# First key products kept plain, weight bits on ScalarE, values double-buffered: one edit of a fused attention and MoE kernel

## The chip, the cores and the metric

One core of a Trainium2 chip runs the whole program. The metric is device microseconds from launch to end; lower is better. TensorE (PE) multiplies matrices, VectorE (DVE), ScalarE (ACT) and GpSimd (POOL) work element by element, and SyncE (SP) only issues DMA transfers here. Each engine executes its own instructions in the order in which the program was written, so a waiting instruction holds up everything behind it on that engine.

## What is computed

Three layers in a row, all in float32:

```python
# 1. delta-rule attention, 4 batches x 8 heads, 768 tokens, head size 48
k_n = k / (norm(k) + 1e-06)
for t in range(768):
    y[t]  = q[t] @ state
    v_old = state.T @ k_n[t]
    state = state + beta[t] * outer(k_n[t], v[t] - v_old)
# 2. gated MLP: x is (3072, 384), d_ff 2048
h = x @ w_in;  x = (h * sigmoid(1.702 * h)) @ w_out
# 3. four dense experts of width 1024, mixed by normalised domain_probs
out += p[:, e:e+1] * (relu(x @ w1[e]) @ w2[e])
```

## The kernel before, in words

**Attention.** The 768 tokens are cut into 12 chunks of 64 (`u`, 0 to 11), and two chunks form a batch `w` (0, 2, 4, ...). For each chunk TensorE forms the products of keys with keys (`queue_g`, L523) in two halves of eight head groups, and VectorE keeps the 32x32 diagonal blocks of them (`keep_d`, L558) in a scratch buffer `GG`, while the off-diagonal blocks are copied out to `G` (`keep_x`). The blocks are turned so that each of the 128 partitions holds one 32x32 triangle, the triangle is inverted row by row, and it is turned back (`to_rows`, L639). For the later batches this inversion runs on GpSimd (`queue_inverse`, L597: 30 steps of two operations, L619 and L621). For batch 0 it runs on VectorE (`queue_first_inverse`, L644): two 16x16 triangles side by side in 14 steps (L674, L676), which are then merged by two rounds of small matmuls (`first` L718, `out1`, `second` L727, `out2` L732). A chunk then solves for its update, reads its output `y` and updates the state (`queue_chain`, L754).

The key norms come from `queue_keys` (L365): a square on ScalarE (L393), a sum (L396) and a chain of about 14 small VectorE operations (L408 to L433) that ends in `rates`. For batch 0 the diagonal blocks are multiplied by a constant mask `cmask` on their way out of PSUM (chunk 0: L564, each half in four pieces of 32 partitions; chunk 1: L571, each half in one piece). For later batches `premask` (L511) builds mask times weight beforehand and `keep_d` multiplies by that.

**Scratch.** Four buffers `scr` (L323) are handed out by `claim`. The squares, `GG`, the turned triangle `X` (kept until both chunks of the batch have solved), the turned copy `d` of the first inverse, and a part of `y` on its way out (`YS`) all live there.

**Weights of the MLP.** The 16 weight tiles arrive as 64-bit numbers, 128x1536 words each. `queue_w1` (L251) turns each into a float32 pair: `small` (L286, ScalarE) and `low` (L289, VectorE, a shift right by 29) work on the two words, `shift` (L293, VectorE) joins them, `hi` (L298, ScalarE) rounds and `lo` (L301, VectorE) keeps the remainder.

**MLP and experts.** The token tiles `t` have 512 columns. For tile 0 and tile 1 the first layer starts on half tiles (256 columns) as soon as one chunk's `y` is there (`HALVED`, `items` L1133, `split_stage` L1142). Each of the 16 (MLP) or 8 (expert) steps `f` is nine matmuls into `ph` (L1013), a gate on ScalarE and VectorE (L1123, L1125, L1126) and nine matmuls into `px` (L1108). The experts (L1279 on) follow when attention is over.

**What sets the order.** The order of the program is not written out by hand. A planner (`Order` and `Task`, L28 to L147) keeps a clock for each engine, a cost, a priority `prio` (lower goes first) and dependencies for each task, and writes a task's instructions at the moment when its clocks say that the task could start. Tasks that name two engines go to the one that would end first, with a bonus for the first named. `can` says when a scratch buffer or PSUM bank is free. MLP matmuls drive the clock (`tick`, L68), attention tasks are slipped in between, and `until` (L76) lets attention run freely while the MLP has to wait. SP's DMA queue is one of the engines ("HW"). What the chip then does differs from the planner's clocks, but the order on each engine stays as written.

Of the kernel before, what the change touches and what calls it, by code (L numbers as in the profile page):

```python
# [9 lines left out]
I32 = mybir.dt.int32  # L10
AF = mybir.ActivationFunctionType
# [5 lines left out]
C = 64  # L17
SB = 32
# [6 lines left out]
GW = 1  # L25
# [62 lines left out]
class Task:  # L88
    def __init__(self, order, fn, eng, cost, deps, lat, prio, slack, can, extra):
        self.o, self.fn, self.lat, self.prio, self.slack, self.can = order, fn, lat, prio, slack, can  # L90
        self.engs = dict(zip(eng, cost)) if isinstance(eng, tuple) else {eng: cost}
        self.pe = eng == "PE"
        self.extra = extra
# [36 lines left out]
    def issue(self):  # L130
# [13 lines left out]
        if len(self.engs) > 1:  # L144
            self.fn(e)
        else:
            self.fn()  # L147
# [3 lines left out]
def delta_attention_moe_moe_kernel(  # L151
# [55 lines left out]
    cmask = ap_.tile([128, SB], F32, name="cmask")  # L207
# [43 lines left out]
    def queue_w1(f, after):  # L251
# [111 lines left out]
    NR = {}  # L363
# [88 lines left out]
    def queue_q(u):  # L452
# [8 lines left out]
        lq = task(load, "HW", 1.32, (edone.get(u - 2), normed[u] if u > 1 else None), lat=4.8, prio=p if u < 4 else p - 30, slack=5)  # L461
        ends, visits, masks = [], [], []
        whole = 1 if u < 2 else 2
        for o in range(2):
# [18 lines left out]
            if len(visits) == whole:  # L483
                t = task(lambda fs=tuple(visits): weave(fs), "PE", 1.0 if whole == 1 else 1.3,
                         (*placed[u], lq, begun[0], *(ends[-1:] if u > 1 else ())), prio=p + 1,
                         can=lambda: None if u > 1 and not od.moe else some_free(banks(), whole))
                for c, f in masks:
                    c.setdefault("end", []).append(task(f, "DVE", 0.6, (t,), prio=p + 1))
                    ends.append(c["end"][-1])
# [16 lines left out]
    def queue_premask(us):  # L506
# [11 lines left out]
        premasked[w] = task(premask, ("POOL", "DVE"), (1.2 * len(us), 0.6 * len(us)), (normed[w],), prio=p,  # L518
# [4 lines left out]
    def queue_g(u):  # L523
# [6 lines left out]
        whole = 1 if u < 4 else 2  # L530
        for o in range(2):
# [3 lines left out]
            def gram(o=o, cell=cell, flip=flip):  # L535
# [4 lines left out]
                for i in range(8):  # L540
                    g = 2 * i + o
                    if u < GW:
                        for x in range(2):
                            d, r = DR[x], TR[x]
                            mm(ps[r:r + C, i, :], lhsT=kr[d:d + D, g, :], rhs=kr[d:d + D, g, :], start=True, stop=True)
                            yield
                        continue
# [10 lines left out]
            def keep_d(x, o=o, cell=cell, flip=flip):  # L558
                if w not in GG:
                    GG[w] = scr[claim(SCR, gheld[w]["end"])][:, 0:2 * NP * SB].rearrange("p (g i) -> p g i", i=SB)  # L560
                a = rows(o)[0]
                if u < GW:
                    for r in range(0, 128, SB):
# [814 lines left out]
```

## Time and profile before

| | |
|---|---|
| median of 3 runs | 1409.41 us (1405.75 to 1409.59) |
| the profiled execution, its own time | 1406.45 us |
| its span, first to last instruction | 1404.7 us |
| PE busy | 1354.4 us (96%) |
| VectorE, ScalarE, GpSimd busy | 617.5, 421.2, 202.5 us |
| TensorE clock granted, mean | 0.991 |

The rows below come from one profiled execution. Times are microseconds from the start of the span. "L564" is line 564 of the kernel; "out<-in" names the tiles. In a timeline, the first number is the start, the second the time from the first to the end of the last of the merged instructions, and a bracket gives idle time of that engine just before and what ended it. A busy share says how full an engine is in a stretch and not whether it sets the end.

### The profile page before, as it was taken

How to read it: one execution, taken by the hardware profiler on the slowest of the kernel's cores; microseconds unless marked ns; L12 is line 12 of the kernel's file. 1: busy time of each engine (PE TensorE's matmuls, PEld its weight loads, DVE VectorE, ACT ScalarE, POOL GpSimd, SP SyncE). 2: the span in 40 equal slices, each digit the busy share in tenths (PEclk: the TensorE clock that was granted, in tenths of full speed). 3: DMA queues.
4: the chain of work that ended last, by engine and by line, in shares of the span. 5: the costliest groups of instructions: out<-in, count | busy, mean ns of one | idle time of the engine just before them, and what ended most of it. 6: DMA issues, size and time to landing. Idle time of an engine off the chain costs nothing.

```text
span 1404.7 us, 29499 instructions
## 1 busy us (share of the span) xinstructions
PE 1354.4 (96%) x13072; PEld 1144.5 (81%) x13072; DVE 617.5 (44%) x1035; ACT 421.2 (30%) x797; POOL 202.5 (14%) x355
## 2 busy tenths in 40 slices
PE   5699999998999999999999999999999999999998
PEld 4588789986878788878888888888888888888888
DVE  7879466474363423323333224443233433233343
ACT  2564344352342434422222112222122222111111
POOL 3057543603507200000000000000000000000000
PEclk9999989999999999999999999999999999999999
DMA  8550131222020103201100001010001000011111
GB/s 222 171 173 17 28 96 40 61 62 61 12 61 7 39 5 134 68 0 29 33 30 30 8 1 30 31 38 31 1 19 30 31 31 8 0 30 31 31 30 46
DMA packets 53696, 63.39 MB, mean 45 GB/s; under 512 B 37120, under 2 KB 38592, under 8 KB 53568
## 3 DMA queue, kind: packets, MB, share of 16 engines
q1 hardware_dynamic: 53568, 61.50, 15.4%
q8 instruction: 102, 1.67, 0.5%
q14 instruction: 26, 0.21, 0.1%
HBM read 52.58 MB, written 7.91 MB: 43 GB/s over the span
## 4 chain that ended last, share of the span: by engine, by line
PE 92%; DVE 4%; issue 2%; DMA 1%; ACT 1%; SPq 0%; DVEq 0%; ACTq 0%
PE ph L1013 42%; PE po L1235 23%; PE px L1108 14%; PE po L1265 5%; PE y L849 2%; PE ch L820 1%; PE gp L550 1%; PE ch L806 1%; PE ch L872 1%; PE ch L835 1%; PE gp L473 1%; DMA rw<-in_w_dram 1%; DMA k<-in_k_dram 0%; ACT su L183 0%; DMA kt<-in_kt_dram 0%
## 5 line engine op out<-in xcount | busy, mean ns | idle before, releaser
L1013 PE MATMUL ph<-xs,w 128*128 128x512 f32 (+1 forms) x2808 | 657.5, 377 | 3.6 <-ACT xs L183 2.0
L1013 PEld LDWEIGHTS ph<-xs,w 128*128 128x128 f32 x2808 | 504.1, 190 | 96.7 <-ACT xs L183 2.1
L1296 DVE SCALAR_TENSOR_TENSOR hh<-ph,hh 128x512 fp32r<-128x512 f32 x192 | 132.5, 690 | 503.4 <-ACT hh L1295 503.4
L1235 PE MATMUL po<-hh,w 128*128 128x512 f32 x1440 | 352.4, 389 | 0.0
L1235 PEld LDWEIGHTS po<-hh,w 128*128 128x128 f32 x1440 | 270.4, 188 | 56.0
L1295 ACT ACTIVATE hh<-ph 128x512 fp32r<-128x512 f32 x192 | 114.9, 598 | 616.6 <-PE ph L1013 616.6
L1108 PE MATMUL px<-gh,w 128*128 128x512 f32 (+1 forms) x1080 | 231.6, 354 | 2.3 <-DVE gh L1126 2.1
L1108 PEld LDWEIGHTS px<-gh,w 128*128 128x128 f32 x1080 | 177.3, 190 | 30.4 <-DVE gh L1126 3.0
L1126 DVE TENSOR_TENSOR gh<-ph,gh 128x512 fp32r<-128x512 f32 (+1 forms) x120 | 69.9, 582 | 149.0 <-ACT gh L1125 147.8
L1123 ACT ACTIVATE ph<-ph 128x512 f32<-128x512 f32 (+1 forms) x120 | 59.6, 497 | 184.9 <-PE ph L1013 179.8
L621 POOL TENSOR_TENSOR scr<-scr,itmp 128x30 f32<-128x30 f32 (+9 forms) x150 | 85.0, 567 | 11.8
L619 POOL TENSOR_TENSOR itmp<-scr 128x30 f32<-128x30 f32 (+9 forms) x150 | 80.4, 536 | 11.1
L1265 PE MATMUL po<-w,hh 128*128 128x384 f32 x384 | 73.9, 342 | 0.0
L1265 PEld LDWEIGHTS po<-w,hh 128*128 128x128 f32 x384 | 69.3, 188 | 2.4
L1125 ACT CAST gh<-ph 128x512 fp32r<-128x512 f32 (+1 forms) x120 | 60.2, 502 | 3.8
L183 ACT COPY su<-ch 64x384 f32<-64x384 f32 (+2 forms) x85 | 38.1, 458 | 49.9 <-PE ch L820 48.5
L1095 DVE TENSOR_TENSOR xs<-x,xs 128x512 fp32r<-128x512 f32 x72 | 45.3, 684 | 0.0
L1094 ACT CAST xs<-x 128x512 fp32r<-128x512 f32 x72 | 39.7, 619 | 0.0
L813 DVE TENSOR_TENSOR v<-v,ch 128x384 f32<-128x384 f32 (+1 forms) x56 | 30.1, 551 | 17.5 <-PE ch L835 5.1
L478 DVE TENSOR_TENSOR pq<-gp,pmask 64x512 f32<-64x512 f32 x48 | 33.1, 689 | 5.9 <-PE gp L473 5.1
L243 DVE TENSOR_TENSOR w<-raw,w 128x768 fp32r<-128x768 f32 x32 | 30.7, 958 | 10.3 <-ACT w L242 9.5
L768 POOL TENSOR_TENSOR v<-v,nr 128x768 f32<-128x768 f32 x9 | 13.3, 1479 | 127.2 <-DMA v<-in_v_dram 119.1
(118 smaller groups left out, 765.8 us busy)
## 6 DMA issues: line engine op xcount, KB each, us to landing
raw<-in_we_dram SPq DMA_DIRECT2D x32, 384.0 KB, 3.0
rw<-in_w_dram SPq DMA_DIRECT2D x14, 768.0 KB, 5.7
raw<-prd SPq DMA_DIRECT2D x20, 256.0 KB, 3.2
kt<-in_kt_dram SPq DMA_DIRECT2D x24, 192.0 KB, 5.1
k<-in_k_dram SPq DMA_DIRECT2D x12, 384.0 KB, 6.1
pq<-in_q_dram SPq DMA_DIRECT2D x24, 192.0 KB, 4.2
v<-in_v_dram SPq DMA_DIRECT2D x12, 384.0 KB, 3.1
out_dram<-oacc SPq DMA_DIRECT2D x80, 48.0 KB, 1.7
```

The costliest lines, as they stand in the source:

```text
L619: E.tensor_tensor(out=tv, in0=x[:, j:j + 1, j + 1:].broadcast_to([128, m, r]), in1=x[:, 0:m, j:j + 1].broadcast_to([128, m, r]), op=ALU.mult)
L621: E.tensor_tensor(out=x[:, 0:m, j + 1:], in0=x[:, 0:m, j + 1:], in1=tv, op=ALU.add)
L1013: mm(ps, lhsT=w[:, a, kk * 128:(kk + 1) * 128], rhs=xs[kk][:, b, cs], start=kk == 0 and i == 0, stop=kk == KD - 1 and i == 2)
L1095: nc.vector.tensor_tensor(out=s[:, 1, :], in0=src, in1=s[:, 0, :].bitcast(F32), op=ALU.subtract)
L1108: mm(px[d][:, cs], lhsT=w[:, a, 384 + d * 128:384 + (d + 1) * 128], rhs=gh[:, b, 0:cs.stop - cs.start], start=f == 0 and i == 0 and cs.sta ...
L1123: a = task(lambda: nc.scalar.activation(out=ph, in_=ph, func=AF.Gelu_apprx_sigmoid), "ACT", 0.05 + 0.43 * c, (pe,), **kw)
L1125: a = task(lambda: nc.scalar.copy(out=hi, in_=ph), "ACT", 0.05 + 0.43 * c, (a,), **kw)
L1126: a = task(lambda: nc.vector.tensor_tensor(out=lo, in0=ph, in1=hi.bitcast(F32), op=ALU.subtract), "DVE", 0.07 + 0.53 * c, (a,), **kw)
L1235: mm(po[kk], lhsT=w[:, a, 384 + kk * 128:384 + (kk + 1) * 128], rhs=hh[:, c, :], start=f == 0 and i == 0, stop=f == F2 - 1 and i == 2)
L1265: mm(ps, lhsT=hh[:, a, b * 128:(b + 1) * 128], rhs=w[:, c, 384:768].rearrange("p (k a i) -> p a k i", a=4, k=KD), start=f == 0 and i == 0, ...
L1295: nc.scalar.activation(out=hh[:, 0, :], in_=ph, func=AF.Relu)
L1296: nc.vector.scalar_tensor_tensor(out=hh[:, 1, :], in0=ph, scalar=0.0, in1=hh[:, 0, :].bitcast(F32), op0=ALU.max, op1=ALU.subtract)
```

## The change

- **First keys.** For chunks 0 and 1 the key products are formed as for later chunks (both halves woven, on all four quadrants), and the diagonal blocks are copied out of PSUM unmasked, by ScalarE or VectorE (`keep_raw`). Mask and weight come together in a tile `m`, made by GpSimd or VectorE (`weigh`) once the norms are there, and are multiplied in after the turn (`clear`, which also clears one more corner).
- **Constants.** The masks and zeroed tiles are made by eight GpSimd tasks of the planner, in the order j, q0, pm, h, su, st, q1, g. `cmask` is gone. What uses one of them names it as a dependency. The helpers' home is a tile `spare` in a weight slot.
- **Low bits.** `low` moves from VectorE (shift right) to ScalarE (scale by 2^-29, rounded down).
- **Values.** `v` has two buffers, so chunk u's load follows the solve of chunk u-2. From chunk 2 on VectorE alone scales `v`; for chunks 0 and 1 GpSimd or VectorE.
- **Scratch.** Three buffers instead of four.
- **Planner's figures.** Several costs, among them the GpSimd inverse (factor 1.5 to 1.2 for batch 2, 1.0 to 0.95 for later ones).

```diff
         def low():
-            nc.vector.tensor_scalar(out=cell["lo"], in0=cell["lo"], scalar1=29, scalar2=None,
-                                    op0=ALU.logical_shift_right)
+            nc.scalar.activation(out=cell["lo"].bitcast(U32), in_=cell["lo"].bitcast(U32), func=AF.Copy, scale=2.0 ** -29 * (1 - 2.0 ** -16),
+                                 bias=7.5 * 2.0 ** -16 - 0.5)
...
-            b = task(low, "DVE", 0.6, (dep, begun[0]), **kw)
+            b = task(low, "ACT", 0.9, (dep, begun[0]), **kw)
...
-    scr = [ap_.tile([128, NP * C], F32, name=f"scr{i}") for i in range(4)]
+    scr = [ap_.tile([128, NP * C], F32, name=f"scr{i}") for i in range(3)]
...
-    SCR = (0, 1, 2, 3)
+    SCR = (0, 1, 2)
...
-        lq = task(load, "HW", 1.32, (edone.get(u - 2), normed[u] if u > 1 else None), lat=4.8, prio=p if u < 4 else p - 30, slack=5)
+        lq = task(load, "HW", 1.32, (edone.get(u - 2), normed[u] if u > 1 else zeros[f"q{u}"]), lat=4.8, prio=p if u < 4 else p - 30, slack=5)
...
-        whole = 1 if u < 4 else 2
+        whole = 1 if u in (2, 3) else 2
...
+            def keep_raw(e, x, o=o, cell=cell, flip=flip):
                 if w not in GG:
                     GG[w] = scr[claim(SCR, gheld[w]["end"])][:, 0:2 * NP * SB].rearrange("p (g i) -> p g i", i=SB)
                 a = rows(o)[0]
-                if u < GW:
-                    for r in range(0, 128, SB):
-                        V.tensor_tensor(out=GG[w][r:r + SB, o:NP:2, :] if not u else GG[w][r:r + SB, NP + o:2 * NP:2, :], in0=cell["ps"][r:r + SB, :, r % C:r % C + SB],
-                                        in1=cmask[r:r + SB].unsqueeze(1).broadcast_to([SB, 8, SB]), op=ALU.mult)
-                    return
                 r, n = (0, 128) if x is None else (TR[x], C)
                 s = 0 if x is None else half(x, flip)
...
+                copy(e, GG[w][r:r + n, c * NP + o:(c + 1) * NP:2, :], cell["ps"][s:s + n, :, a:a + SB])
...
-            last = task(lambda j=j: step(j), "POOL", (0.52 + 0.0037 * m) * (1.5 if w == 2 else 1.0), (last,), prio=p)
+            last = task(lambda j=j: step(j), "POOL", (0.52 + 0.0037 * m) * (1.2 if w == 2 else 0.95), (last,), prio=p)
...
+        def weigh(e):
+            bt = BT[w].rearrange("p (h i) -> p h i", h=2)
+            cell["m"] = spare[:, H * H:3 * H * H].rearrange("p (h a b) -> p h a b", h=2, a=H)
+            for h in range(2):
+                (V if e == "DVE" else nc.gpsimd).tensor_tensor(
+                    out=cell["m"][:, h], in0=jmask, in1=bt[:, h].unsqueeze(1).broadcast_to([128, H, H]), op=ALU.mult)
+
         def clear():
 
             x = cell["x"]
-            bt = BT[w].rearrange("p (h i) -> p h i", h=2)
-            V.tensor_tensor(out=x, in0=x, in1=bt.unsqueeze(2).broadcast_to([128, 2, H, H]), op=ALU.mult)
+            V.tensor_tensor(out=x, in0=x, in1=cell["m"], op=ALU.mult)
             V.memset(X[w][:, H:, 0:H], 0.0)
+            V.memset(X[w][:, 0:H, H:], 0.0)
             V.memset(X[w].rearrange("p i j -> p (i j)")[:, 0:SB * SB:SB + 1], 1.0)
...
         begun[w] = task(begin, "DVE", 2.0, ds, prio=p, can=lambda: any_free(SCR))
-        last = task(clear, "DVE", 1.1, (begun[w],), prio=p)
+        last = task(weigh, ("POOL", "DVE"), (1.2, 0.9), (normed[w], zeros["j"]), prio=0)
+        last = task(clear, "DVE", 1.4, (begun[w], last), prio=p)
...
-        before = [solved2[u - 1, hu] for hu in range(2) if (u - 1, hu) in solved2]
+        before = [solved2[u - 2, hu] for hu in range(2) if (u - 2, hu) in solved2]
...
-            V2[u] = ap_.tile([128, NP, D], F32, name="v2", tag="v2")
+            V2[u] = ap_.tile([128, NP, D], F32, name="v2", tag="v2", bufs=2)
...
-        lv = task(scale_v, ("POOL", "DVE"), (1.9, 0.97), (lv, normed[u]), prio=p + 1)
+        lv = task(scale_v, ("DVE",) if u > 1 else ("POOL", "DVE"), (0.97,) if u > 1 else (1.5, 0.97), (lv, normed[u]), prio=p + 1)
...
+        for n, fn, cost in (("j", set_j, 0.5), ("q0", lambda: E_.memset(PQ[0], 0.0), 1.85), ("pm", set_p, 1.95),
+                            ("h", set_h, 0.9), ("su", lambda: E_.memset(SU, 0.0), 1.4),
+                            ("st", lambda: E_.memset(stage, 0.0), 1.4), ("q1", lambda: E_.memset(PQ[1], 0.0), 1.85),
+                            ("g", set_g, 1.1)):
+            zeros[n] = task(fn, "POOL", cost, (), prio=2)
+        od.clk["POOL"] = 0.8
```

## Rows read from the trace of the kernel before

**Rows 1.** Busy time by stretch: length, PE, PEld, DVE, ACT, POOL, PEclk, DMA share, GB/s.
```profile
0.00:33.07 33.07, 16.00 (x320) 14.55 (x320) 24.12 (x67) 8.69 (x15) 12.68 (x36) 1.00 0.86 227
33.07:66.39 33.32, 19.41 (x865) 17.53 (x865) 27.70 (x56) 17.92 (x36) 2.69 (x1) 1.00 0.51 166
66.39:100.00 33.61, 32.97 (x764) 29.84 (x766) 24.94 (x44) 26.03 (x54) 13.76 (x23) 0.95 0.59 183
100.00:126.00 26.00, 23.44 (x323) 22.30 (x318) 25.53 (x38) 11.66 (x25) 24.04 (x26) 0.93 0.22 48
...
168.00:189.00 21.00, 16.73 (x423) 13.69 (x419) 9.13 (x16) 8.04 (x18) 18.43 (x32) 0.76 0.31 84
...
335.00:600.00 265.00, 264.87 (x2978) 214.56 (x2977) 108.70 (x180) 99.72 (x181) 70.00 (x127) 1.00 0.14 43
```

**Rows 2.** Timeline of VectorE, 11 to 31 us.
```profile
11.03 1.61 DVE L408 TENSOR_SCALAR scr<-scr 128x32 int32<-128x32 int32 x1
...
16.15 1.68 DVE L564 TENSOR_TENSOR scr<-gp,cmask 32x256 f32<-32x256 f32 x4
17.86 0.42 DVE L571 TENSOR_TENSOR scr<-gp,cmask 128x256 f32<-128x256 f32 x1
...
20.29 1.15 DVE L666 TENSOR_TENSOR scr<-scr,bt 128x512 f32<-128x512 f32 x1
...
29.52 0.69 DVE L681 TENSOR_TENSOR scr<-scr,bt 128x512 f32<-128x512 f32 x1
```

**Rows 3.** Timeline: first merge, on TensorE, ScalarE and TensorE again.
```profile
33.22 1.90 PE L718 MATMUL gp<-scr,scr 32*32 32x16 f32 x128 [10.94 <-ACT rw L286]
...
34.91 0.83 ACT L393 ACTIVATE scr<-k 128x768 f32<-128x768 f32 x1
35.77 0.37 ACT L183 COPY scr<-gp 128x256 f32<-128x256 f32 x1
...
39.53 1.57 PE L727 MATMUL gp<-scr,scr 32*32 32x16 f32 x99 [2.73 <-issue]
```

**Rows 4.** Chain and timeline: chunk 2's output lands, tile 1 starts; inverse of batch 2.
```profile
174.27 2.33 DMA stage<-scr
...
180.40 2.07 PE ph L1013 x8
...
132.75 1.92 POOL L625 TENSOR_TENSOR scr<-scr,bt 128x1024 f32<-128x1024 f32 x1
...
149.59 2.23 DVE L642 STREAM_TRANSPOSE scr<-scr 128x1024 f32<-128x1024 f32 x1
```

**Rows 5.** Timeline: GpSimd beside L408, and L408 of the next batch.
```profile
10.80 1.81 POOL L1046 MEMSET pq<- 128x2048 f32 x1
...
54.27 0.18 DVE L408 TENSOR_SCALAR scr<-scr 128x32 int32<-128x32 int32 x1
```

**Rows 6.** Timeline, 60 to 67 us: GpSimd, VectorE, ScalarE.
```profile
60.26 2.69 POOL L514 TENSOR_TENSOR scr<-gmask,bt 128x1024 f32<-128x1024 f32 x1 [39.37 <-DVE bt L432]
61.69 1.68 DVE L289 TENSOR_SCALAR rw<-rw 128x768 int32<-128x768 int32 x1
...
65.14 0.91 ACT L298 CAST w<-rw 128x768 fp32r<-128x768 f32 x1 [3.04 <-DVE rw L293]
66.07 0.60 ACT L183 CAST xs<-y 128x128 fp32r<-128x128 f32 x3
```

**Rows 7.** Groups by line, 66.39 to 126 us: count, busy us, mean ns, idle before.
```profile
L289 DVE TENSOR_SCALAR rw<-rw 128x768 int32<-128x768 int32 x9 | 5.9, 652 | 0.0
...
L286 ACT ACTIVATE rw<-rw 128x768 f32<-128x768 f32 x7 | 6.3, 921 | 0.0
```

**Rows 8.** Timeline and chain: square of chunk 4, turn of batch 2, solve of chunk 1.
```profile
80.65 0.85 ACT L393 ACTIVATE scr<-k 128x768 f32<-128x768 f32 x1
...
82.50 2.04 DVE L610 STREAM_TRANSPOSE scr<-scr 128x1024 f32<-128x1024 f32 x1
...
92.78 0.47 PE ch L820 x32
```

More of the change, by code (lines that the diff above doesn't have):

```diff
@@ L24 @@
 PE_SHARE = 0.8
-GW = 1
 class Order:
@@ L361, in delta_attention_moe_moe_kernel @@
     direct = {}
-    NR = {}
+    NR, zeros = {}, {}
+    spare = wp.tile([128, 1536], F32, name="sp", tag=f"w{RAW - 1}")
+    jmask = spare[:, 0:SB * SB // 4].rearrange("p (a b) -> p a b", a=SB // 2)
     def queue_keys(us):
@@ L558, in keep_d @@
             def keep_d(x, o=o, cell=cell, flip=flip):
+                a = rows(o)[0]
+                r, n = (0, 128) if x is None else (TR[x], C)
+                s = 0 if x is None else half(x, flip)
+                gg = GG[w][r:r + n, c * NP + o:(c + 1) * NP:2, :]
+                V.tensor_tensor(out=gg, in0=cell["ps"][s:s + n, :, a:a + SB], in1=gg, op=ALU.mult)
+            def keep_raw(e, x, o=o, cell=cell, flip=flip):
                 if w not in GG:
@@ L689, in queue_first_inverse @@
                 marks.append(last)
-            last = task(lambda j=j: step(j), "DVE", 0.26 + 0.0042 * j * (H - 1 - j), (last,), prio=p)
+            last = task(lambda j=j: step(j), "DVE", 0.4 + 0.003 * j * (H - 1 - j), (last,), prio=p)
         last = task(end, "DVE", 0.6, (last,), prio=p)
@@ L1039, in delta_attention_moe_moe_kernel @@
-        nc.gpsimd.memset(PQ[0], 0.0)
-        for r in range(0, 128, SB):
-            for o in range(2):
-                nc.gpsimd.affine_select(out=pmask[r:r + SB, o], in_=m2[r:r + SB], pattern=[[1, C]], compare_op=ALU.is_gt,
-                                        fill=0.0, base=-(r % C ^ SB * o), channel_multiplier=-1)
-        nc.gpsimd.memset(SU, 0.0)
-        nc.gpsimd.memset(stage, 0.0)
-        nc.gpsimd.memset(PQ[1], 0.0)
-        od.clk["POOL"] = 9.5
+        H = SB // 2
+        E_ = nc.gpsimd
@@ new lines, in delta_attention_moe_moe_kernel, with set_j, set_g @@
+        ones, minus = spare[:, 1024:1024 + C], spare[:, 1024 + C:1024 + C + SB]
+        def set_j():
+            E_.memset(minus, -1.0)
+            E_.affine_select(out=jmask, in_=minus[:, 0:1].unsqueeze(2).broadcast_to([128, H, H]), pattern=[[-1, H], [1, H]],
+                             compare_op=ALU.is_gt, fill=0.0, base=0, channel_multiplier=0)
+        def set_g():
+            for r in range(0, 128, SB):
+                at = slice(r, r + SB)
+                E_.affine_select(out=gmask[at], in_=minus[at], pattern=[[-1, SB]], compare_op=ALU.is_gt,
+                                 fill=0.0, base=0, channel_multiplier=1)
@@ new lines, in set_h, with set_p @@
+        def set_h():
+            E_.memset(hmask, -1.0)
+            for r in range(0, 128, SB):
+                at = slice(r, r + SB)
+                E_.affine_select(out=hmask[at], in_=hmask[at], pattern=[[0, 1]], compare_op=ALU.is_ge,
+                                 fill=0.0, base=H - 1, channel_multiplier=-1)
+        def set_p():
+            E_.memset(ones, 1.0)
+            for r in range(0, 128, SB):
+                for o in range(2):
+                    E_.affine_select(out=pmask[r:r + SB, o], in_=ones[r:r + SB], pattern=[[1, C]], compare_op=ALU.is_gt,
+                                     fill=0.0, base=-(r % C ^ SB * o), channel_multiplier=-1)
```

46 lines of the change are left out of this document (12 added, 34 removed).

## The prediction

> **What bounds the kernel now.** I read first the table by stretch [rows 1]. From 335 to 600 us TensorE works 264.87 of 265 us at a granted clock of 1.00: it is the bound, and only time in which it stands still or runs slowly can be won. Three places show such time. In the opening (0 to 66.39 us, up to the first MLP matmul) TensorE works 16.00 + 19.41 of 66.39 us, while VectorE works 24.12 + 27.70. From 66.39 to 126 us TensorE idles 0.64 + 2.56 us and the clock averages 0.95 and 0.93; in the second half of that VectorE is busy 25.53 of 26.00 us. From 168 to 189 us TensorE idles 4.27 us at a mean clock of 0.76.
>
> Next I read the timelines, for what holds TensorE in these places. In the opening it is one VectorE chain: L408, the masked copies L564 and L571, the turn, the clear L666, the steps, L681 [rows 2], two more turns, and then the merge matmuls start at 33.22 us [rows 3]. At 168 us it is MLP tile 1, which needs chunk 2's output: its last pieces land at 176.60 us, and the matmuls start at 180.40 [rows 4]. Why so late? GpSimd finished the inverse of batch 2 at 134.67 us (132.75 + 1.92), but VectorE turned it back only at 149.59 [rows 4]. The planner had written the turn that late, since it costs this inverse with a factor of 1.5. Some 15 us lie unused in this chain, and the stop of TensorE hangs on it.
>
> **The change part by part.** 0.3% of the median is 4.2 us, about what a measurement of this kernel can tell from no change.
>
> *First keys.* Between the norms and the turn stand four L564 and one L571, from 16.15 to 18.28 us [rows 2]: 2.1 us leave the chain. In their place come six plain copies, which need only the products and can lie beside the norms. ScalarE is named first for them, and it is busy 8.69 of the first 33.07 us [rows 1]; I cost them at nothing. If that cover fails and three fall to VectorE, they cost 3 x 0.42 = 1.3 us, by L571. Chunk 0 needs twice as many small matmuls as before, on a TensorE that is idle 17 of those 33 us: nothing. The tile `m` is made on GpSimd during the turn: nothing. If it fell to VectorE, its two half-size products would cost about one L681, 0.7 us.
>
> *The clear.* Its product took 1.15 us, while L681 of the same size took 0.69 [rows 2]. With `m` ready I expect 0.69, but one memset is added. Bounds -0.5 and 0, taken -0.2.
>
> *Constants.* L408 took 1.61 us here [rows 2] and 0.18 on the next batch [rows 5]. It ended at 12.64, and the GpSimd memset beside it at 12.61 [rows 5]: it was held by it. In the new order this long memset runs before four short mask pieces, so about one microsecond goes. Bounds -1.43 and 0, taken -1.0. The Trainium skill, "SBUF — State Buffer", section "Who interferes with whom", says that VectorE in a two-port mode and GpSimd hold their shared port as a lock, and that whoever comes second waits out the whole instruction of the other. By that rule L408 would wait for one short piece at most, and the term would be near its bound of -1.43.
>
> *SP's queue.* Loads of q now wait in the planner for their zeroed tile, so the loads behind them (chunk 0's values, the first weights) are issued earlier. Chunk 1's values move ahead of the later weights, which start later by one such load. Nothing, either way: VectorE takes up the first weight only after the inverse.
>
> *Scratch.* With three buffers the square of chunk 2 can't run before the first merge. So it no longer stands in front of the merge's copy, which began at 35.77, behind L393, while its matmuls had ended at 35.12 [rows 3]. A `low` of 0.9 us may stand there instead. Bounds -0.6 and +0.3, taken -0.3. The norms of batch 2 come later by the squares' new place, an estimate of 2 to 3 us (two squares of 0.83 and their sums). L514, which ends that chain, was over at 62.95 [rows 6], and batch 2 is turned at 82.50 [rows 8], with four products in between: covered.
>
> *Low bits.* VectorE loses 16 instructions and ScalarE gains 16. The nearest row for the new price is L286, with the same tile and engine: 0.92 us [rows 7]. One of the old ones sits badly: L289 took 1.68 us beside GpSimd's L514, and ScalarE stood 3.04 us in front of a weight that waited for this, with the conversion of chunk 1's `y` behind it [rows 6]. Bounds -3.0 (all that idle time) and 0; taken halfway, -1.5. From 66.39 to 126 us nine of them, 5.9 us, leave a VectorE that is full in the second half [rows 1, 7]. TensorE can win at most its 3.2 us of idle time and the low clock's share, 0.05 x 33.61 + 0.07 x 26.00 = 3.5 us; I take -2. ScalarE gets nine of 0.92 us. With seven of them (as many as L286 has there) before 100 us it comes to 26.03 + 6.4 = 32.5 of 33.61 us, and the MLP's gates queue behind them: +1. Stretch together -1; bounds -4 and +8.3.
>
> The Trainium skill, "ScalarE: Activation LUTs", section "Rules for kernel authors", speaks against this part: additions and products belong on VectorE, which is the faster per element. The trace agrees on durations, 0.65 against 0.92 us [rows 7]. By that rule the part costs 16 x 0.27 = 4.3 us of engine time, and the sum would be smaller by up to that; by the rows it is paid on the emptier engine.
>
> *Values.* Chunk 1's values are scaled on an idle GpSimd, off the path: nothing. From chunk 2 on, one product of 128x768 per chunk moves to VectorE, which is busy 109 of 265 us there [rows 1]: nothing.
>
> *Planner's figures.* By the formula the 30 steps of this inverse cost 30 x 0.52 + 0.0037 x 4960 = 34 us; a factor of 1.2 instead of 1.5 brings L642 forward by 10.2 us on the planner's clock. From the end of the turn of batch 2 (84.54 [rows 8]) to L642 the chip took 65 us, where the planner counted 51 + 2.4. So it is 12 us on the chip: to about 137 us, just behind GpSimd's end. Then chunk 2's output lands before tile 0 is over, and the stop goes. It is worth 4.27 us of idle time and 0.24 x 21 = 5.0 us of low clock, at most 9.3 us [rows 1]. Attention work that ran inside the stop has still to be done. Taken -7, bounds -9.3 and 0.
>
> *Sum.* Opening -2.1 - 0.2 - 1.0 - 0.3 - 1.5 = -5.1; stretch to 126 us -1; stop -7. Together -13.1 from the profiled execution's 1406.45 us: 1393.4. That execution lies 3.0 us under the median of the three runs, 1409.41; going halfway, I predict **1395 us**.
>
> **The rivals.**
>
> *The stop stays (0.24).* With three buffers the square of chunk 4 (80.65 us) can take the last free one just ahead of the turn of batch 2 (82.50) [rows 8]. The turn then waits for the solve of chunk 1, whose matmuls ended at 93.25: 10.7 us, which eat what the planner's factor gave. For it: the square did come first before. Against it: its priority is the weaker, and ScalarE, which executes it, is fuller now. Then -5.1 - 1 = -6.1 remains, in medians about 1402 us.
>
> *ScalarE becomes the bound (0.10, slower).* It works in order, and each `low` stands in front of gates, state copies and conversions. Its idle time from 66.39 to 100 us was 7.6 us [rows 1], of which my count leaves 1.1; if a late weight or copy uses that up, TensorE waits for every further `low`. With all 16 on the path it is 16 x 0.92 = 14.7 us, and chunk 2 is as late as before, so the stop stays: 1406.45 - 5.1 + 14.7 = 1416, in medians about 1417. The skill's rule for ScalarE leads here.
>
> *The opening isn't VectorE's (0.08).* Between two merge matmuls TensorE stood 2.73 us for nothing that the profile shows [rows 3]. If its instructions come at a pace of their own, an earlier turn only lengthens such stops. With the stop at 168 us left as well, -1 remains: in medians about 1407 us.
>
> **How the numbers follow.** The forecast has 0.58. Low end: the opening with every bound -2.1 - 0.5 - 1.43 - 0.6 - 3.0 = -7.6, the stretch -4, the stop -9.3, from 1406.45: 1385.5, taken 1386. High end: 1408, which takes in the first and the third rival and leaves out ScalarE's 0.10 and a few hundredths around it. Faster than 1405.2 us: the forecast and five sixths of the first rival, 0.78. Within 0.3%: the rest of that and the third, 0.12. Slower than 1413.6 us: 0.10.
>
> **What would show it.** Right, step by step: L408's successor takes well under 1 us; the merge matmuls start by 30 us and the first MLP matmul near 61; batch 2 is turned back within 3 us of GpSimd's last step; TensorE goes from tile 0 into tile 1 without a stop and at a clock of 1.00. Wrong: a turn of batch 2 that starts only after chunk 1's solve; ScalarE over 95% busy for 30 us behind the first MLP matmul, with TensorE waiting for gates; or several microseconds of idle TensorE at the change of tiles.

## The result, and the profile after

| | before | after |
|---|---|---|
| median | 1409.50 us (4 runs, 1405.75 to 1410.40) | 1387.82 us (4 runs, 1387.02 to 1389.33) |
| the profiled execution, its own time | 1406.45 us | 1388.16 us |
| its span | 1404.7 us | 1386.5 us |
| PE busy | 1354.4 us | 1342.3 us |
| TensorE clock granted, mean | 0.991 | 0.998 |

The ratio is 0.9852, with an interval from 0.9833 to 0.9872: faster by 1.5%. Between the two profiled executions the difference is 18.3 us.

To see where the time went, both executions are cut at the same places of the program: the first full run of MLP matmuls, the store of each of the finished MLP tiles 0 to 3 (the moves of `x1d`), and the end. Two of these stretches in the table by stretch of the kernel before, tile 0 and tile 2 (length, PE, PEld, DVE, ACT, POOL busy, clock, DMA share, GB/s):

```profile
67.05:194.57 127.52, 119.44 (x2357) 103.82 (x2358) 89.32 (x149) 63.27 (x134) 80.52 (x126) 0.94 0.26 74
...
292.45:383.98 91.53, 86.69 (x1224) 69.15 (x1222) 44.59 (x79) 32.69 (x64) 33.72 (x63) 0.96 0.18 43
```

The same two of the kernel after:

```profile
64.38:181.00 116.62, 113.54 (x2339) 98.03 (x2343) 83.19 (x141) 63.48 (x133) 76.06 (x124) 0.99 0.32 82
...
274.50:361.74 87.24, 87.16 (x1438) 69.48 (x1437) 50.02 (x86) 33.05 (x65) 30.34 (x55) 1.00 0.20 50
```

| stretch | before | after | difference |
|---|---|---|---|
| opening, to the first full MLP run | 67.05 | 64.38 | -2.67 |
| tile 0 | 127.52 | 116.62 | -10.90 |
| tiles 1 to 3 | 273.21 | 268.30 | -4.91 |
| the rest | 936.92 | 937.20 | +0.28 |

Tile 0 carries most of it: TensorE's idle time there falls from 8.08 to 3.08 us, and the granted clock rises from 0.94 to 0.99, worth about 0.06 x 127.5 - 0.01 x 116.6 = 6.5 us. Within tiles 1 to 3, tile 1 is 4.4 us shorter, tile 2 4.3 us shorter and tile 3 3.8 us longer.

The rows of after that answer to those of before. First, the table by stretch [rows 1]:

```profile
0.00:30.47 30.47, 9.40 (x384) 7.89 (x384) 20.15 (x60) 10.81 (x20) 14.79 (x32) 1.00 1.01 257
30.47:64.40 33.93, 21.87 (x930) 19.50 (x930) 28.30 (x55) 27.80 (x49) 2.69 (x1) 1.00 0.60 204
64.40:100.00 35.60, 35.00 (x810) 31.85 (x811) 25.61 (x45) 27.79 (x56) 18.31 (x30) 0.95 0.53 144
100.00:126.00 26.00, 24.32 (x354) 22.72 (x355) 24.25 (x45) 11.63 (x24) 23.49 (x33) 1.00 0.17 36
...
168.00:189.00 21.00, 20.86 (x427) 18.76 (x426) 16.90 (x27) 9.51 (x22) 3.04 (x5) 1.00 0.53 144
...
335.00:600.00 265.00, 263.76 (x2972) 213.19 (x2971) 114.72 (x181) 100.39 (x184) 67.39 (x124) 1.00 0.15 46
```

The stop from 168 to 189 us is gone: 20.86 of 21.00 us at a clock of 1.00, where it was 16.73 at 0.76. The timeline of the chain behind it, VectorE and GpSimd [rows 4, 8]; L607, L622 and L639 are the turn, the last step and the turn back of batch 2 (L610, L625 and L642 before):

```profile
77.41 2.03 DVE L607 STREAM_TRANSPOSE scr<-scr 128x1024 f32<-128x1024 f32 x1
125.03 1.92 POOL L622 TENSOR_TENSOR scr<-scr,bt 128x1024 f32<-128x1024 f32 x1
...
131.13 2.08 DVE L607 STREAM_TRANSPOSE scr<-scr 128x1024 f32<-128x1024 f32 x1
133.86 2.21 DVE L639 STREAM_TRANSPOSE scr<-scr 128x1024 f32<-128x1024 f32 x1
```

The turn back begins at 133.86 instead of 149.59 us, 6.9 us behind GpSimd's end at 126.95. Of these 15.7 us, 7.7 come from GpSimd, which ends that much earlier (batch 2 is turned 5.1 us earlier, at 77.41 instead of 82.50), and 8 from the place of the turn back in VectorE's order. Just before it VectorE turns batch 4 (131.13); that place becomes important below. The opening on VectorE and GpSimd [rows 2, 5], then on TensorE and ScalarE:

```profile
10.93 0.96 POOL L1039 TENSOR_SCALAR_AFFINE_SELECT gmask<-sp 32x32 f32<-32x32 f32 x4
11.30 0.18 DVE L410 TENSOR_SCALAR scr<-scr 128x32 int32<-128x32 int32 x1
...
15.19 1.97 DVE L657 STREAM_TRANSPOSE scr<-scr 128x1024 f32<-128x1024 f32 x1
16.59 1.48 POOL L773 TENSOR_TENSOR v<-v,nr 128x768 f32<-128x768 f32 x1
17.26 1.36 DVE L669 TENSOR_TENSOR scr<-scr,sp 128x512 f32<-128x512 f32 x1
18.62 0.27 DVE L670 MEMSET scr<- 128x256 f32 x1
18.90 0.27 DVE L671 MEMSET scr<- 128x256 f32 x1
...
13.25 0.21 PE L550 MATMUL gp<-kt 48*32 48x32 f32 x1 [3.89 <-issue]
...
14.02 1.13 ACT L184 COPY scr<-gp 128x256 f32<-128x256 f32 x3 [2.22 <-PE gp L550]
```

L410 (L408 before) takes 0.18 instead of 1.61 us, the turn follows the norms with no masked copies between, but the clear, L669, takes 1.36 us: GpSimd's scaling of `v` (L773) runs beside it until 18.07 us. The turn no longer waits for the norms alone. TensorE stands 3.89 us in the key products of the first batch, ScalarE's plain copies come behind that and end at 15.15 us, and the turn starts at 15.19, where the norms had ended at 15.06. Here that costs 0.1 us; in other executions of this opening the copies came 0.6 us (`a_again`), 1.4 (`a_low_dve`) and 1.9 us (`a_hold4`) behind the norms. Then the first merge, on TensorE and ScalarE [rows 3]:

```profile
30.62 1.90 PE L723 MATMUL gp<-scr,scr 32*32 32x16 f32 x128 [6.32 <-DVE rw L267]
...
32.58 0.89 ACT L286 ACTIVATE rw<-rw 128x768 f32<-128x768 f32 x1 [0.18 <-DMA rw<-in_w_dram]
33.37 0.86 ACT L289 ACTIVATE rw<-rw 128x768 uint32<-128x768 uint32 x1
34.26 0.37 ACT L184 COPY scr<-gp 128x256 f32<-128x256 f32 x1
...
36.59 0.71 PE L732 MATMUL gp<-scr,scr 32*32 32x16 f32 x35 [0.45 <-issue]
```

The merge starts 2.6 us earlier, and the stop of TensorE within it that is put down to nothing is 0.45 instead of 2.73 us. Its copy stands behind two pairs of `small` and `low` (L286, L289), until 34.26, though the matmuls had ended at 32.52. Last, the wait in front of the MLP [rows 6], on GpSimd, VectorE (the two L293 each in a narrow window of its own, since a wide one merges them), ScalarE and TensorE:

```profile
59.75 2.69 POOL L516 TENSOR_TENSOR scr<-gmask,bt 128x1024 f32<-128x1024 f32 x1 [29.39 <-DVE bt L434]
...
60.58 2.67 DVE L293 SCALAR_TENSOR_TENSOR rw<-rw 128x768 int32<-128x768 int32 x1
...
63.18 0.95 DVE L293 SCALAR_TENSOR_TENSOR rw<-rw 128x768 int32<-128x768 int32 x1
64.05 0.67 DVE L871 TENSOR_TENSOR xs<-y,xs 128x128 fp32r<-128x128 f32 x3
...
61.42 0.60 ACT L184 CAST xs<-y 128x128 fp32r<-128x128 f32 x3
61.90 0.95 ACT L286 ACTIVATE rw<-rw 128x768 f32<-128x768 f32 x1
...
61.74 0.38 PE L1018 MATMUL ph<-xs,w 128*128 128x256 f32 x1 [0.39 <-ACT xs L184]
64.38 3.81 PE L1018 MATMUL ph<-xs,w 128*128 128x256 f32 x17 [2.25 <-DVE xs L871]
```

ScalarE converts `y` at 61.42 instead of 66.07 us, 4.65 earlier, and one MLP matmul starts at 61.74. But VectorE's half of the conversion (L871) stands behind two L293, and the first of them takes 2.67 us where the second takes 0.95. Beside it runs GpSimd's mask product for batch 2, L516, until 62.44 us: the same product (L514 then) that held VectorE's L289 in the kernel before. The L286 that the second L293 needs is over at 62.85, before the first L293 ends at 63.26, so ScalarE is not what it waits for. TensorE stands 2.25 us and starts the full run only 2.67 us earlier than before.

### The profile page after: what moved, and what is told of

It reads as the page before. It is cut to its first block, busy times and chain, and to the rows that moved or that the text cites. A ratio compares the mean times of both kernels' runs of the same rounds, so it can differ in the third digit from the quotient of the medians.

```text
span 1386.5 us, 29623 instructions
## 1 busy us (share of the span) xinstructions
PE 1342.3 (97%) x13136; PEld 1131.6 (82%) x13136; DVE 614.6 (44%) x1020; ACT 432.3 (31%) x814; POOL 198.0 (14%) x345
## 4 chain that ended last, share of the span: by engine, by line
PE 93%; DVE 2%; issue 1%; ACT 0%; DVEq 0%
PE ph L1018 43%; PE po L1249 24%; PE px L1122 14%; PE po L1279 5%; PE y L854 2%; PE ch L825 1%; PE ch L811 1%; PE gp L546 1%; PE ch L877 1%; PE gp L475 1%; PE ch L840 1%; DVE pq L480 0%; PE y L853 0%; PE gp L550 0%; DVE gh L1140 0%
## 5 line engine op out<-in xcount | busy, mean ns | idle before, releaser
L184 ACT COPY su<-ch 64x384 f32<-64x384 f32 (+2 forms) x79 | 34.9, 457 | 70.3 <-PE ch L825 69.7
L1258 DVE TENSOR_TENSOR oacc<-oacc,po 128x512 f32<-128x512 f32 x45 | 30.9, 688 | 1.5
```

## The experiments

Ratios are to the kernel before on the same chip, whose medians were 1405.85 us (beside `b_factor`, `a_factor_old`, `a_low_dve`, `b_keys_later`), 1407.82 (`a_again`, `a_low_guard`, `a_keys_masked`, `b_scr3`), 1406.94 (`a_hold4`, `a_hold3`, `a_v_old`) and 1407.27 (`a_hold4_dve`). Variants from different chips are compared by their ratios. The changed kernel was run once more:

> The changed kernel once more, beside the other three on one chip, so that their medians can be compared with it. Both theories: 1386 to 1391 us.

Measured: 1389.68 us, ratio 0.9870 [0.9847, 0.9893]. Variants of it are compared with this.

### The planner's factors

`b_factor`: the kernel before, with the two new factors and nothing else.

```diff
-(1.5 if w == 2 else 1.0)
+(1.2 if w == 2 else 0.95)
```

> The kernel before with the planner's two factors of the change alone (1.5 to 1.2 for the inverse of batch 2, 1.0 to 0.95 for the later ones). Theory: the stop of TensorE at the change from tile 0 to tile 1 hangs on where the planner writes the turn back of batch 2, so L642 comes within 3 us of the end of L625, the stop goes, and the time falls by 4 to 9 us, to 1400 to 1405 us. Rival: the stop went because the whole opening and the weights came earlier; then the factor alone leaves the time at 1407 to 1411 us.

Measured: 1397.01 us, ratio 0.9939 [0.9920, 0.9959], 8.6 us less. The turn back came at 135.79 us, 13.8 us earlier than before's and 1.9 us behind GpSimd's end. The row of the table by stretch:

```profile
168.00:189.00 21.00, 21.00 (x416) 18.39 (x415) 14.85 (x27) 10.87 (x25) 16.19 (x30) 1.00 0.63 158
```

`a_factor_old`: the reverse edit, in the changed kernel.

> The changed kernel with the planner's old factors (1.5 and 1.0). Theory: the turn back of batch 2 is again written late, 10 us or more behind the end of GpSimd's inverse, TensorE stops at the change of tiles, and the time is 4 to 9 us above the changed kernel, 1392 to 1397 us. Rival: the other parts carry the gain at the change of tiles, 1387 to 1390 us.

Measured: 1393.78 us, ratio 0.9914 [0.9890, 0.9939]: against 0.9870 that is 0.44%, 6 us more. The turn back came at 139.79 us, 12.4 us behind GpSimd's end (127.39), and the stop was back:

```profile
168.00:189.00 21.00, 18.96 (x394) 17.01 (x395) 11.97 (x21) 10.05 (x24) 2.41 (x3) 0.84 0.46 120
```

So the factors alone are worth 6 to 9 us, by the mechanism that the prediction gave.

### Low bits and scratch buffers

`a_low_dve`: the changed kernel with the low bits back on VectorE.

```diff
-            nc.scalar.activation(out=cell["lo"].bitcast(U32), in_=cell["lo"].bitcast(U32), func=AF.Copy, scale=2.0 ** -29 * (1 - 2.0 ** -16),
-                                 bias=7.5 * 2.0 ** -16 - 0.5)
+            nc.vector.tensor_scalar(out=cell["lo"], in0=cell["lo"], scalar1=29, scalar2=None,
+                                    op0=ALU.logical_shift_right)
...
```

> The changed kernel with the low bits back on VectorE, as the shift it was. Theory (terms of the forecast): moving them was worth 2.5 us, 1.5 in the opening and 1 behind it, so this takes 1389 to 1392 us. Rival A: VectorE executes the same work faster (0.55 against 0.9 us) and ScalarE delays the conversions, so this takes 1383 to 1387 us. Rival B: VectorE's fullness and its blocking beside GpSimd are the larger part of the gain, 1393 us or more.

Measured: 1397.20 us, ratio 0.9941 [0.9923, 0.9960], some 10 us more than the changed kernel. The size is that of the rival, but not its mechanism. The timeline, ScalarE and VectorE:

```profile
73.53 0.87 ACT L395 ACTIVATE scr<-k 128x768 f32<-128x768 f32 x1
...
89.87 2.05 DVE L607 STREAM_TRANSPOSE scr<-scr 128x1024 f32<-128x1024 f32 x1
```

The square of chunk 4 ran at 73.53 us instead of 99.67 and took the last of three scratch buffers; the turn of batch 2 came at 89.87 instead of 77.41, right behind the end of chunk 1's solve on TensorE (89.64), and the stop returned (18.39 of 21.00 us busy, clock 0.77). To part the two causes, `a_low_guard` keeps the low bits on VectorE and makes that square depend on the turn of batch 2:

```diff
-(lk, turns[0] if w == 2 else None, *sqs[-1:])
+(lk, turns[0] if w == 2 else over.get(2) if w == 4 else None, *sqs[-1:])
...
+        over[w] = b
```

> The changed kernel with the low bits back on VectorE, as in the run before, and one dependency more: the square of chunk 4 may not take a scratch buffer before batch 2 is turned. Theory (the scratch collision, not the engine of the low bits, made the earlier run slow): batch 2 is turned well before chunk 1's solve, GpSimd ends near 130 us, no stop at 168 us, clock 1.00 there, and the time is within 3 us of the changed kernel's. Rival (VectorE carrying the low bits is the cost): it stays 8 to 12 us above the changed kernel.

Measured: 1389.07 us, ratio 0.9868 [0.9846, 0.9890], the changed kernel's within the measurement. Its timeline:

```profile
81.97 2.03 DVE L607 STREAM_TRANSPOSE scr<-scr 128x1024 f32<-128x1024 f32 x1
...
85.96 0.84 ACT L395 ACTIVATE scr<-k 128x768 f32<-128x768 f32 x1
```

So the engine of the low bits is worth nothing at the end that can be measured; what `a_low_dve` lost was the scratch buffer. (The guard alone in the changed kernel wasn't run; there the square comes behind the turn anyway.) At the start of the MLP the low bits do show: in `a_low_guard` L289 on VectorE takes 2.27 us beside L516, and the first full run starts at 65.67 us, 1.0 us later than in `a_again` (64.63). `b_scr3` shows the collision in the kernel before:

```diff
-    SCR = (0, 1, 2, 3)
+    SCR = (0, 1, 2)
```

> The kernel before with three scratch buffers handed out and nothing else changed. Theory (scratch rival's mechanism): the square of chunk 4 takes the last buffer, batch 2 is turned only after chunk 1's solve, 8 to 12 us later than before's 82.5 us, chunk 2's output comes as much later, the stop at the change of tiles grows, and the time is 3 to 10 us above before. Rival (the planner's late turn back leaves 15 us of slack that takes this up): GpSimd ends by 146 us, the turn back stays near 150, and the time is within 1.5 us of before.

Measured: 1426.46 us, ratio 1.0131 [1.0109, 1.0153], 18.6 us more, about twice what I expected at most. Square, turn and turn back in the timeline:

```profile
81.03 0.84 ACT L393 ACTIVATE scr<-k 128x768 f32<-128x768 f32 x1
...
94.78 2.13 DVE L610 STREAM_TRANSPOSE scr<-scr 128x1024 f32<-128x1024 f32 x1
...
158.15 2.25 DVE L642 STREAM_TRANSPOSE scr<-scr 128x1024 f32<-128x1024 f32 x1
```

The turn is 12.3 us later than before's and starts right behind chunk 1's solve (its matmuls end at 94.71 us). The 15 us between GpSimd's end (143.10) and the turn back stay, so they don't take the delay up, and TensorE is busy 28.24 us between 160 and 200 us at a clock of 0.70, where it was 35.58 us at 0.87. Whether all 18.6 us belong to this one turn wasn't shown: the square of chunk 2 too runs later, at 52.35 instead of 34.91 us. With three buffers the time hangs on which of two tasks, the square or the turn, comes first.

### First keys

`a_keys_masked`: the changed kernel with the first keys of before (old products for chunk 0, masked copies on VectorE, weights in the clear, no `m`). GpSimd builds `cmask` in addition, in the place of the helper for `m`.

```diff
-            halves.append((cell, gram, keep_d if w else keep_raw, keep_x))
+            halves.append((cell, gram, keep_d, keep_x))
...
-        last = task(weigh, ("POOL", "DVE"), (1.2, 0.9), (normed[w], zeros["j"]), prio=0)
...
```

> The changed kernel with the first keys as before: products of chunk 0 in the old form, masked copies on VectorE, weights multiplied in by the clear, no m. Theory (my term): the first merge matmul starts 2 to 2.5 us later than the changed kernel's 30.6 us, the first full MLP matmul 1 to 2.5 us later, and the end 1 to 3 us later. Rival (the start of the MLP hangs on the first weight, not on the merge): the merge is late by the same, but the MLP starts within 0.5 us and the end is within 1 us.

Measured: 1393.26 us, ratio 0.9898 [0.9873, 0.9922]; 3.6 us above the changed kernel by medians, 2.6 by spans. GpSimd, VectorE and TensorE in the timeline:

```profile
11.30 1.81 POOL L1076 MEMSET pq<- 128x2048 f32 x1
...
11.58 1.57 DVE L412 TENSOR_SCALAR scr<-scr 128x32 int32<-128x32 int32 x1
...
21.62 0.69 DVE L677 TENSOR_TENSOR scr<-scr,bt 128x512 f32<-128x512 f32 x1
...
28.61 1.57 POOL L779 TENSOR_TENSOR v<-v,nr 128x768 f32<-128x768 f32 x1 [11.41 <-DMA v<-in_v_dram]
...
28.88 1.39 DVE L685 TENSOR_TENSOR itmp<-scr 128x72 f32<-128x72 f32 x1
...
35.28 1.90 PE L729 MATMUL gp<-scr,scr 32*32 32x16 f32 x128 [10.81 <-DVE rw L269]
```

The merge came 4.7 us later than in after, twice what I expected. Only about 2.0 us of that are the masked copies between the norms and the turn. 3.3 us are GpSimd beside VectorE at three places: the additional mask work pushed the long memset beside L412, held by it as in the kernel before (1.4 us), and the two scalings of `v` (L779) hold one small product of the norm chain, L436 (0.96 instead of 0.19 us), and one of the inverse, L685 (1.39 instead of 0.23). The clear gives 0.9 us back, since here GpSimd was done (L677). The first full MLP run came at 70.97 us, 6.3 us after that of `a_again` (64.63), yet only 2.6 to 3.6 of these were left at the end. The rival, that the merge doesn't matter, falls. The size of the term is confirmed in the chain; what it is worth at the end this run can't say, since most of its delay is GpSimd's.

### The stop at 326 us

Beyond tile 0 the kernel before lost time where I had not looked. On TensorE, timeline of before:

```profile
330.77 0.33 PE L554 MATMUL gp<-kt 48*32 48x32 f32 x7 [4.84 <-issue]
```

TensorE stands 4.84 us in the middle of the key products of batch 8 for nothing that the profile shows; from 320 to 335 us its clock is 0.81. In after these 15 us are fully busy at 1.00. In before the loads of batch 10's keys run beside it. `b_keys_later` holds these loads until batch 8 is turned, by one-column writes of VectorE into their targets:

```diff
+        late = task(lambda: [V.memset(t, 0.0) for u in us for t in (KT[u % 4][:, 0, 0:1], K2t[u % NK][:, 0:1])], "DVE", 0.28, (edone.get(w - 4), edone.get(w - 3), over[w - 2]), prio=1) if w == 10 else None
...
-(edone.get(u - 4), normed.get(u - 2))
+(edone.get(u - 4), normed.get(u - 2), late)
...
```

> The kernel before, where the loads of keys for batch 10 are held, by four one-column writes on VectorE, until batch 8 has been turned. Theory: the stop of 4.84 us at 325.9 us comes from the transfers of these keys, which run while TensorE goes through the many small matmuls of batch 8's key products; with the loads behind them the stop is under 1 us and the time falls by 4 to 7 us, to 1402 to 1406 us. Rival: the stop belongs to these matmuls themselves and stays at 4 to 5 us, 1407 to 1411 us.

Measured: 1406.76 us, ratio 0.9992 [0.9972, 1.0013], no gain. The stop shrank and didn't go:

```profile
326.96 0.33 PE L554 MATMUL gp<-kt 48*32 48x32 f32 x7 [2.15 <-issue]
```

So the loads can be at most a part of the cause. What the two stops share is another transfer. The page counts, beside the kernel's own DMA queue, one that it calls "instruction" (before: packets, MB, share):

```profile
q8 instruction: 102, 1.67, 0.5%
```

The trace keeps the time of each of its packets, of 16 KiB. Divided among them, TensorE's 26,220 matmuls and weight loads are 257 per packet, and after's 26,343 with 103 packets are 256, so this queue goes with TensorE's instructions. In before one packet started at 328.24 us, 2.3 us into the stop, while the key loads filled the DMA engines (share 1.21 from 328 to 329 us); it landed at 329.33, and TensorE went on at 330.77. In `b_keys_later` the packet started before the stop, at 324.06, and landed at 325.74; TensorE went on 1.23 us later. From 10 us on the 14 traces have 56 stops of TensorE that are longer than 1.2 us and put down to "issue"; every one of them ends 1.22 to 1.63 us after such a packet has landed. The reading that fits all 56 is that TensorE stood because its next instructions weren't there. That the key loads made the packet late in before fits its late start, but only this one pair of runs speaks for it.

The price of the stop stays open. In `b_factor` it is gone as well, yet tiles 1 to 3 are only 0.9 us shorter than before's (from 184.28 to 456.56 us).

### The new wait ahead of the MLP

`a_hold4` and `a_hold3` try to take the L293 out of the way of the conversion, by writing the work on weights 4 (or 3) and later only after chunk 0's `y` is converted:

```diff
-            a = task(small, "ACT", 0.83, (dep,), **kw)
+            dep = (dep, ydone[0] if f >= 4 else None)
+            a = task(small, "ACT", 0.83, dep, **kw)
...
```

> The changed kernel with one dependency more: from weight 4 on, the two steps on the raw words (small, low) are written only after chunk 0's y is converted. Theory (the wait that took the place of the removed one: the conversion of y stands behind weight work on ScalarE and VectorE): the last conversion ends near 61 instead of 64.05 us, the first full run of MLP matmuls starts 2 to 3.5 us earlier than 64.4 us, and the end comes 1 to 3 us earlier. Rival (the MLP then waits for weights that come too late): the run starts earlier, but TensorE idles or loses clock by as much between 66 and 126 us, and the time is the same or up to 5 us longer.

> The same with the dependency from weight 3 on: one weight less is ready when the MLP starts. Theory: the start as in the run with weight 4, within 0.5 us, and the end within 1 us of that run. Rival (weights too late): 2 to 6 us longer than that run, with TensorE waiting for a weight's parts behind 66 us.

Measured: 1402.51 us, ratio 0.9965 [0.9945, 0.9985], and 1402.82 us, ratio 0.9979 [0.9962, 0.9996]. Both expectations fell, except that the two end alike. With weight 4 the norm chain of batch 2 and its mask product, now on VectorE (L517, 62.94 to 64.12 us), slipped ahead of the conversion, and the run starts at 64.50 us. With weight 3 it starts 4 us earlier:

```profile
60.43 2.56 PE L1019 MATMUL ph<-xs,w 128*128 128x256 f32 x17 [0.40 <-DVE xs L872]
```

Yet both are some 13 us slower than `a_again`. Late weights don't explain it: tile 0, which needs them, ends at 179.67 and 178.31 us, before the 181.00 of the changed kernel. The larger part of the loss is in tile 1, which ends at 283.79 and 281.88 us instead of 274.50; by the spans another 4.0 and 6.6 us follow behind it. The timeline of `a_hold4`, GpSimd and VectorE:

```profile
130.92 1.92 POOL L623 TENSOR_TENSOR scr<-scr,bt 128x1024 f32<-128x1024 f32 x1
132.80 1.92 POOL L517 TENSOR_TENSOR scr<-gmask,bt 128x1024 f32<-128x1024 f32 x1
...
182.64 2.05 DVE L608 STREAM_TRANSPOSE scr<-scr 128x1024 f32<-128x1024 f32 x1
```

With the new order the mask of batch 4 went to GpSimd, behind the inverse of batch 2. It missed its place ahead of the turn back, chunks 2 and 3 went first, and batch 4 was turned 51.5 us later than in the changed kernel (131.13). In `a_hold3` VectorE made this mask, but at 136.49 us, also behind the turn back (129.56), and batch 4 was turned at 188.10 us. `a_hold4_dve` gives the mask to VectorE:

```diff
-("POOL", "DVE"), (1.2 * len(us), 0.6 * len(us))
+("DVE",) if w == 4 else ("POOL", "DVE"), (0.6 * len(us),) if w == 4 else (1.2 * len(us), 0.6 * len(us))
```

> The run that held the weights from weight 4 on, and in it the mask times weight of batch 4 is given to VectorE alone, as in the changed kernel, where GpSimd took it behind the inverse of batch 2. Theory (what that run lost was the turn of batch 4, 182.64 instead of 131.13 us, which came behind the turn back of batch 2 and all of chunk 2's and 3's solves): batch 4 is turned before 150 us, tile 1 ends within 3 us of the changed kernel's 274.50 us, and the time is 1386 to 1391 us. Rival (holding the weights cost the time itself): still 1398 to 1404 us, with the same late end of tile 1.

Measured: 1390.31 us, ratio 0.9877 [0.9855, 0.9898]. The mask and the turn of batch 4:

```profile
129.34 1.20 DVE L517 TENSOR_TENSOR scr<-gmask,bt 128x1024 f32<-128x1024 f32 x1
...
141.38 2.00 DVE L608 STREAM_TRANSPOSE scr<-scr 128x1024 f32<-128x1024 f32 x1
```

The theory holds: 12 us hang on the place of one 1.2 us instruction, here ahead of the turn back (132.69 us). And holding the weights, with the MLP's first full run at 63.55 us, one microsecond earlier than in `a_again`, brings nothing at the end.

### Values

`a_v_old`: the changed kernel with one buffer for `v`, its old load, and GpSimd or VectorE to scale it.

```diff
-        lv = task(scale_v, ("DVE",) if u > 1 else ("POOL", "DVE"), (0.97,) if u > 1 else (1.5, 0.97), (lv, normed[u]), prio=p + 1)
+        lv = task(scale_v, ("POOL", "DVE"), (1.9, 0.97), (lv, normed[u]), prio=p + 1)
...
```

> The changed kernel with v as before: one buffer, its load behind the solve of the chunk before, scaled by GpSimd or VectorE with the old cost for all chunks. Theory (my term, nothing): within 2 us of the changed kernel, TensorE's idle time from 189 to 600 us unchanged within 1 us. Rival (the scaled values were a wait that the change took away): 3 us or more longer, with more idle time before the first matmuls of a chunk that read v.

Measured: 1390.25 us, ratio 0.9878 [0.9856, 0.9900]: nothing, as costed. From 189 to 600 us TensorE idles 6.6 us in it and 4.3 in `a_again`, a difference above the 1 us that I allowed, without a trace at the end.

No version here beats the changed kernel by more than the measurement.

## Why the prediction was right, and where it wasn't

The direction and the reason of the largest part were right, and 1387.8 us lies in the range, near its low end. The sum was -13.1 us from the profiled execution; it became -18.3. The stretches that the sum covers, opening and tile 0, came to -13.6; that this is so near is luck, since the opening won 2.4 us less than forecast and tile 0 2.9 us more.

Of the signs named beforehand, L408's successor (0.18 us) and the way from tile 0 into tile 1 (20.86 of 21.00 us busy at 1.00) came. The merge started at 30.62 us, not by 30; a single MLP matmul started at 61.74, near the 61 named, but the full run only at 64.38; and the turn back lay 6.9 us behind GpSimd's end, not within 3. None of the signs of being wrong came.

- **Planner's figures, -7: right.** The turn back moved towards GpSimd's end, the stop went, and the two runs on the factors give 6 to 9 us. Alone, in `b_factor`, they brought the turn back forward by 13.8 us, against 12 in the text; in after half of the 15.7 us is GpSimd's earlier end, which the text did not have. Tile 0 as a whole, stop and stretch, has -10.9 against -8.
- **First keys, -2.1: right in the chain.** From the end of the norms to the turn it was 2.10 us before and 0.13 after. That the additional small matmuls cost nothing held by 0.1 us only: TensorE stopped 3.89 us in them, and elsewhere the turn waited for that, 0.6 us in `a_again`. Their undoing cost 2.6 to 3.6 us at the end, but with 3.3 us of waiting beside GpSimd in it.
- **Constants, -1.0: undersized.** It measured -1.43, the bound. This is the value by the Trainium skill, "SBUF — State Buffer", "Who interferes with whom": an instruction that comes second on the port shared with GpSimd, in VectorE's two-port modes, waits out the other. The trace agrees twice: 1.61 us beside the memset before, 1.57 in `a_keys_masked` (both end within 0.04 us of the memset). In after L410 started beside the four short mask pieces and took 0.18 us, not held at all. That L408 runs in a two-port mode no trace here shows.
- **The clear, -0.2: wrong sign.** It measured 1.36 + 0.27 more for the memset against 1.15, so +0.5. I took 0.69 from L681, a row with GpSimd idle. In after GpSimd's scaling of `v` runs until 18.07 us beside it; in `a_keys_masked` GpSimd was done, and the old form took 0.69. The step that failed is that I put the form of the product down as the cost, and GpSimd's neighbourhood was it: the new form takes 0.69 us as well where GpSimd is done (`a_low_dve`, `a_hold4`). The same section of the Trainium skill says that a VectorE instruction with two inputs in SBUF contends with a GpSimd one that reads it; these rows agree.
- **Scratch and the merge's copy, -0.3: wrong.** The copy waited 1.74 us for ScalarE instead of 0.65, so +1.1, outside my bounds of -0.6 to +0.3. I counted one `low` in front of it; it was two, each with its `small`.
- **Low bits, -1.5 in the opening and -1 to 126 us: nothing at the end.** `a_low_guard` has them on VectorE and the same time; its MLP starts 1.0 us later. The old wait went, as I said (ScalarE's conversion 4.65 us earlier), but another took its place: GpSimd's mask product, which had held L289, now holds L293 for 1.7 us, and VectorE's half of the conversion stands behind that. The step that failed is that I took the slow L289 for a matter of that instruction. Moving it away left its cause, GpSimd's product, beside whatever VectorE does next, and I asked what stands in front of the conversion on ScalarE and not what stands in front of its other half on VectorE. For the stretch to 126 us I had named 3.2 us of idle time and 3.5 us of low clock, 6.7 together, and gave no reason for setting the bound at -4.
- **Opening, -5.1: -2.67.** The end of the second merge came 4.4 us earlier (L737 at 52.02, L732 at 56.41 before); 2.3 of these are the shorter stop in the first merge, which the sum did not have. Then L516 took 1.7 back. `a_hold4_dve` and `a_keys_masked` show, moreover, that microseconds at the start of the MLP arrive only in part at the end.
- **Not in the sum: tiles 1 to 3, -4.9.** The 4.84 us stop at 326 us was in the trace of before, in tile 2, and I had read 335 to 600 us and taken the rest for the same. That it makes up the 4.9 us isn't shown: tile 1 is shorter by as much without such a stop, and `b_factor` lost the stop and gained 0.9 us.

Single undos give 6 (factors), 3.6 (first keys), 0 (low bits) and 0.6 us (values). That is half of the 18 to 22 us; constants, scratch, the other costs and the woven products of queries with keys for chunks 0 and 1 (in the edit, but not in the list of the change) were not undone alone. What is left can't be given to one part: every edit makes the planner write another order, as the last group of runs shows. This stays open.

Of the rivals, the scratch collision was real: `b_scr3` and `a_low_dve` show it, step by step as written, and the second lies 7.5 us above the changed kernel by medians and 10 by the ratios, where the rival had 7 against the forecast. In the changed kernel it didn't come because the square of chunk 4 ran at 99.67 us, 22 us behind the turn; with the low bits on VectorE it ran at 73.53. That is what moving the low bits does here; that ScalarE's fullness is the planner's reason is argued, as the text had it. ScalarE as the bound fell: it was busy 27.79 of 35.60 us behind the first MLP run, not the 32.5 that I had counted. The third, instruction pace in the opening, has a real mechanism, as the packets of the instruction queue show, and it had a part in the opening: the stop of 3.89 us in the key products is new, and the kernel before has none over 1.2 us there. In the merges the stops did not grow as it said: together they fell from 4.36 (2.73 and 1.63) to 2.38 us (0.45 and 1.93).

## What to carry to other kernels

When a planner writes the order from its own clocks, a wrong cost of one task can be worth more than the instructions that are saved, as here; compare, for each long chain on another engine, when it ends on the chip and when its successor was written. With few buffers, ask for each claim which task takes the last one, and tie the order down by a dependency rather than by how busy an engine happens to be. When a VectorE instruction is slow in one place, look at what GpSimd does beside it before its form is blamed. When a wait goes, follow the freed data through every engine that still has to touch it, and ask whether the cause of the wait went too.

## What the runs showed of the hardware

**VectorE beside GpSimd.** A VectorE product of 128x512 took 0.69 us with GpSimd idle, 1.15 us [rows 2] with 0.6 us of a GpSimd product still to run at its start, and 1.36 us with 0.8 us still to run. In all nine traces in which the clear started during GpSimd's product it ended 0.54 to 0.55 us after that product's end. Where VectorE came first (`b_scr3`, 20.36 us), its product took 0.69 us and GpSimd's 1.86 instead of 1.48: whoever comes second waits. L293 took 2.67 us beside L516 and 0.95 right behind it.

**TensorE's instructions.** Mostly in stretches of many small matmuls TensorE stops for 1 to 5 us, put down to "issue" by the profile: 2.73 us [rows 3] and 4.84 us before, 1.93 us in the second merge of after, 3.93 us up to 341.76 us in `b_scr3`. Each of these, like all 56 such stops over 1.2 us in the traces, ends 1.22 to 1.63 us after a 16 KiB packet of the instruction queue has landed. Most of the hundred packets of a run cause no such stop; what makes one late was not tested.
